# Attention over four batches at a time, one group of small products per chunk, ahead of two feed-forward layers on one Trainium2 core

## Chip, cores and metric

The kernel runs on one core of a Trainium2 chip. Its metric is the device time of one execution in microseconds (us). A run's figure is the median over repeated executions, and beside it stands one execution taken with the hardware profiler.

## What is computed

Linear attention with decay (batch B = 4, heads H = 8, sequence S = 768, head width D = 48) feeds two dense layers in fp32 accuracy; its rows become 3072 tokens of width 384.

```python
for t in range(S):
    cur = einsum('bhd,bhe->bhde', u * k[t], v[t])
    y[t] = einsum('bhd,bhde->bhe', r[t], state + cur)
    state = w * state + einsum('bhd,bhe->bhde', k[t], v[t])
x = y.transpose(0, 2, 1, 3).reshape(3072, 384)
h = x @ w_in            # 384 -> 2048
x = (h * cos(h)) @ w_out
g, val = x @ w_gate, x @ w_val   # 384 -> 1536
out = (g * sigmoid(g) * val) @ w_out2
```

The state of one batch and head is a 48 x 48 matrix, and batches do not depend on one another.

## The kernel before, in words

**Attention in chunks.** 128 tokens of one batch make a chunk `c`; there are 24, numbered batch by batch, so chunks 0 to 5 are batch 0. `attn_load` (L226) brings two transfers per chunk: `ch` (r and k by channel, 448 KB) and `tk` (r, k and v by token, 608 KB). Heads go in four pairs `q` of two halves `g`; half 0 lies on partitions 0 to 47 and half 1 on 64 to 111. VectorE scales `ch` with the decay tables (`attn_scale`, L243) and makes the diagonal term (`attn_diag`, L248 to L251). ScalarE writes that diagonal into two `am` tiles (L274, eight instructions). TensorE makes, per chunk, four sorts of small fp32 products; each fp32 product stands in the trace as two records, so 16 records a sort:

- scores (L281): 48 rows of either half against 128 columns, half 0 into PSUM bank `a` and half 1 into bank `b`; VectorE then lays them over `am` above the diagonal (L284, twice).
- growth of the state (L292), into bank `a`; not for the last chunk of a batch.
- old state times r (L298), into bank `x`, with a block-diagonal state of 112 rows; not for the first chunk of a batch.
- output (L314): v times `am`, into bank `x` behind the former.

The state is scaled on ScalarE (L306, four instructions) and added to on VectorE (L310, twice). The result `xo` is copied to `st` (L318 for block 0; L320 and L321 as a high and a low part for later blocks), and SyncE's queue moves it into the block's `x` tile by six transfers for a part (L327 to L332).

**Token blocks.** Four chunks in sequence make a block of 512 tokens (`TB`), six blocks in all. Block 0 is multiplied in plain fp32 with `wf`; later blocks use three reduced-precision products with high and low parts (`mm3`, L170 to L174). The steps of the first layer are pairs (block j, f), f = 0 to 15: `f1_up` (L406) makes 128 features into bank `h` (two banks in turn), a chain of six elementwise instructions turns them into `gh` and `gl` (L420 to L426, L177, L180; in block 0 the last two are left out), and `f1_down` (L435), two steps later, adds them into the three banks `y`.

**Order.** `attn_block` is a generator with four stretches per chunk; `schedule` (L497) takes one stretch after each `f1_up`, so block j+1 is made during the 16 steps of block j, its last output in step 15. Block 0 is made ahead of all steps. `prefix` (L74) comes first: small tables, chunk 0, the raw weights of f = 0 and 1, and a flag on the decays, on which all engines branch. In block 0's steps `conv1` (L133) turns 64-bit weights into fp32 from two raw buffers of 768 KB, and in block 1's steps `split1` splits them into `wt` tiles. The tile framework sorts instructions of a stretch by their readiness at build time, so an engine's order is not quite the program's; each engine then runs its queue in order. The second layer (`f2_up`, `f2_down`) follows from about 545 us on.

Of the kernel before, what the change touches and what calls it, by code (L numbers as in the profile page):

```python
# [18 lines left out]
C = 128  # L19
# [5 lines left out]
G = 256  # L25
# [7 lines left out]
TOKW = 2 * DM + NP * VW  # L33
CHW = 2 * NP * C
# [8 lines left out]
NSLOT = 34  # L43


class Kernel:
# [27 lines left out]
    def prefix(self):  # L74
# [6 lines left out]
        r1 = r0 + CHW + TOKW  # L81
# [18 lines left out]
        w = self.rawbuf[0][0:1, 0:DM]  # L100
# [15 lines left out]
        nc.scalar.activation(out=w, in_=w, func=ACTF.Abs, bias=self.center[:, 0:1])  # L116
        nc.vector.tensor_reduce(out=mx, in_=w, axis=AX.X, op=ALU.max)
        nc.vector.tensor_scalar(out=self.flag, in0=mx, scalar1=0.5 * (self.w_max - self.w_min), scalar2=None,
                                op0=ALU.is_le)
        self.attn_tables(wch)  # L120
        self.attn_scale(0)
        self.attn_ptok()
        self.attn_diag(0)
        self.raw1(0)
# [17 lines left out]
    def bank(self, tag, bufs=1):  # L142
        return self.ps.tile([128, 512], F32, tag=tag, bufs=bufs, name=tag)

# [41 lines left out]
    def attn_open(self):  # L186
        self.ap_guard = self.tc.tile_pool(name="attn", bufs=1)
        self.ap = self.ap_guard.__enter__()
        self.state = None
    def attn_tables(self, wch):  # L190
        nc = self.nc
        pr, pk = self.pr, self.pk
# [6 lines left out]
        while n <= hc:  # L199
            sq = up[:, :, n // 2:n // 2 + 1]  # L200
            nc.vector.tensor_tensor(out=up[:, :, n:n + 1], in0=sq, in1=sq, op=ALU.mult)
            if n < hc:
                nc.vector.tensor_tensor(out=up[:, :, n + 1:2 * n], in0=up[:, :, 1:n],
                                        in1=up[:, :, n:n + 1].to_broadcast([ROWS, NP, n - 1]), op=ALU.mult)
            n *= 2
        nc.vector.reciprocal(out=pk[:, :, hc:C], in_=up[:, :, 1:hc + 1])
        nc.scalar.activation(out=pr[:, :, hc:C], in_=up[:, :, 0:hc], func=ACTF.Copy)
        nc.vector.tensor_copy(out=pk[:, :, 0:hc], in_=up[:, :, hc - 1::-1])
# [17 lines left out]
    def attn_load(self, c, at=None):  # L226
        if c >= NCH or c in self.chunks:
            return
        nc = self.nc
        if at is None:  # L230
            ch = self.ap.tile([ROWS, 2, NP, C], F32, tag="ch", bufs=2, name="ch")
            tk = self.ap.tile([128, TOKW], F32, tag="tk", bufs=2, name="tk")
        else:
            ch = at[0:ROWS, 0:CHW].rearrange("p (a n t) -> p a n t", a=2, n=NP)
            tk = at[:, CHW:CHW + TOKW]
# [3 lines left out]
                          tk[:, 2 * DM:].rearrange("p (n w) -> p n w", n=NP))  # L239

# [13 lines left out]
    def attn_chunk(self, c, x, exact):  # L254
        nc, ap = self.nc, self.ap
        mm = nc.tensor.matmul
        first = c % NC_B == 0
        last = c % NC_B == NC_B - 1
        off = (c % CPB) * C
        ch, rt, kt, v = self.chunks[c]  # L260
        rm, km = ch[:, 0], ch[:, 1]
        if c:
            self.attn_scale(c)
            self.attn_diag(c)
        at = self.at.pop(c)
        if not last:
            nc.vector.tensor_tensor(out=kt, in0=kt, in1=self.ptok, op=ALU.mult)
        self.attn_load(c + 1)
        am = []
        for g in range(2):  # L270
            t = ap.tile([128, NP, C], F32, tag="am", bufs=2, name="am")
            for q in range(NP):
                h = 2 * q + g
                nc.scalar.activation(out=t[:, q], in_=self.ident, func=ACTF.Copy, scale=at[:, h:h + 1])  # L274
            am.append(t)
        yield
        sc = [self.bank(b).rearrange("p (n t) -> p n t", n=NP) for b in "ab"]
        for q in range(NP):
            for g in range(2):
                rows = slice(g * 64, g * 64 + D)  # L280
                mm(sc[g][:, q], lhsT=km[rows, q], rhs=rm[rows, q], start=True, stop=True)  # L281
        mask = self.upper.rearrange("p (o t) -> p o t", o=1).to_broadcast([128, NP, C])
        for g in range(2):
            nc.vector.copy_predicated(am[g], mask, sc[g])  # L284
        yield
        xo = self.bank("x").rearrange("p (n t) -> p n t", n=NP)
        wide = (slice(0, 64), slice(64, VW))
        if not last:
            po = self.bank("a")[:, 0:NP * D].rearrange("p (n d) -> p n d", n=NP)
            for q in range(NP):  # L290
                for g in range(2):
                    mm(po[g * 64:g * 64 + D, q], lhsT=kt[:, (2 * q + g) * D:(2 * q + g + 1) * D],  # L292
                       rhs=v[:, q, g * 64:g * 64 + D], start=True, stop=True)
        old = self.state
        if not first:
            for q in range(NP):
                for g in range(2):
                    mm(xo[wide[g], q], lhsT=old[:, q, wide[g]], rhs=rm[:, q],  # L298
                       start=(q == 0), stop=False)
        if not last:  # L300
            self.state = ap.tile([ROWS, NP, VW], F32, tag="state", bufs=2, name="state")
            if first:
                nc.gpsimd.memset(self.state, 0.0)
            else:
                for q in range(NP):
                    nc.scalar.activation(out=self.state[:, q], in_=old[:, q], func=ACTF.Copy,  # L306
                                         scale=self.w128[:, q:q + 1])
            for g in range(2):
                sv = self.state[g * 64:g * 64 + D, :, g * 64:g * 64 + D]
                nc.vector.tensor_tensor(out=sv, in0=sv, in1=po[g * 64:g * 64 + D], op=ALU.add)  # L310
        yield
        for q in range(NP):
            for g in range(2):
                mm(xo[wide[g], q], lhsT=v[:, q, wide[g]], rhs=am[g][:, q],  # L314
                   start=(first and q == 0), stop=(q == NP - 1))
        st = ap.tile([ROWS, 2, NP, C], F32, tag="st", bufs=1, name="st")
        if exact:
            nc.scalar.activation(out=st[:, 0], in_=xo[0:ROWS], func=ACTF.Copy)  # L318
        else:
            nc.scalar.activation(out=st[:, 0].bitcast(F32R), in_=xo[0:ROWS], func=ACTF.Copy)  # L320
            nc.vector.tensor_tensor(out=st[:, 1].bitcast(F32R), in0=xo[0:ROWS], in1=st[:, 0], op=ALU.subtract)  # L321
        for i in range(1 if exact else 2):
            dst = x if exact else x[:, i].bitcast(F32)
            src = st[:, i]
            put = nc.sync.dma_start
            o = slice(off, off + C)
            put(out=dst[0:D, :, o], in_=src[0:D, 0:KT])  # L327
            put(out=dst[D:2 * D, :, o], in_=src[64:64 + D, 0:KT])
            put(out=dst[96:128, 0, o], in_=src[0:32, KT])
            put(out=dst[96:112, 1, o], in_=src[32:48, KT])  # L330
            put(out=dst[112:128, 1, o], in_=src[64:80, KT])
            put(out=dst[96:128, 2, o], in_=src[80:112, KT])  # L332
        yield

    def attn_block(self, j):
        x = self.xblk[j] = self.xf if j == 0 else self.x_tile()
        for i in range(CPB):
            yield from self.attn_chunk(j * CPB + i, x, j == 0)
# [48 lines left out]
    def general_block(self, j):  # L387
        nc = self.nc
        x = self.xblk[j] = self.xf if j == 0 else self.x_tile()
# [239 lines left out]
```

## Time and profile before

| | |
|---|---|
| median of 3 runs | 993.65 us (993.15 to 995.31) |
| profiled execution | 994.0 us |
| its span, first to last instruction | 992.2 us |
| mean granted TensorE clock | 0.990 of full speed |
| busy: TensorE, VectorE, ScalarE | 959.6, 577.6, 466.8 us |

Busy time of TensorE is a union of intervals whose ends are modelled, since its products overlap. Its rate is better read from start to start of records that follow each other. The stages are the stretch ahead of the first up product (to 46.7 us), block 0 (to about 152 us), blocks 1 to 5 (to about 547 us) and the second layer.

### The profile page before, as it was taken

What the parts mean: (1) busy time and instruction counts of PE and PEld (TensorE: products, weight loads), DVE (VectorE), ACT (ScalarE), POOL (GpSimd) and SP (SyncE); (2) the same over time, 40 slices, a digit from 0 to 9 for tenths busy, and PEclk for the clock granted to TensorE, in tenths of its full rate; (3) what the DMA queues carried; (4) which work ended last, traced back from release to release, by engine and by line L of the source; (5) the groups of instructions that cost most, each with busy time, mean ns of one, the idle gap of its engine ahead of it and who ended that gap; (6) DMA issues with size and microseconds to landing.
All of it is one profiled execution on the core that took longest, in us unless ns stands there. A gap on an engine that the chain in (4) does not pass through costs nothing.

```text
span 992.2 us, 13079 instructions
## 1 busy us (share of the span) xinstructions
PE 959.6 (97%) x4988; PEld 745.1 (75%) x4988; DVE 577.6 (58%) x932; ACT 466.8 (47%) x905; POOL 2.1 (0%) x8
## 2 busy tenths in 40 slices
PE   3899999999999999999899999999999999999997
PEld 2644447777777877877787888888888888888886
DVE  7878897666766667765699873333333333333332
ACT  5676866556555565655699762211211222212111
POOL 0000000000000000000000000000000000000000
PEclk9799999999999999999999999999999999999999
DMA  6675524225224132321763601101001001000001
GB/s 216 193 246 172 170 65 151 64 76 161 63 62 149 54 94 68 124 60 31 257 191 118 232 1 46 51 1 63 34 1 64 32 1 64 32 1 9 25 0 36
DMA packets 50393, 86.21 MB, mean 87 GB/s; under 512 B 7057, under 2 KB 24338, under 8 KB 50322
## 3 DMA queue, kind: packets, MB, share of 16 engines
q1 hardware_dynamic: 50322, 85.29, 27.0%
q8 instruction: 41, 0.67, 0.3%
q14 instruction: 30, 0.25, 0.1%
HBM read 62.46 MB, written 14.16 MB: 77 GB/s over the span
## 4 chain that ended last, share of the span: by engine, by line
PE 80%; DVE 7%; DMA 6%; SPq 2%; ACT 2%; issue 1%; ACTq 0%; DVEq 0%
PE y L172 10%; PE h L172 10%; PE h L173 10%; PE h L174 10%; PE y L173 10%; PE y L174 10%; DMA region<-in_w 2%; PE b L174 2%; PE a L174 2%; PE a L172 2%; PE b L172 2%; PE b L173 2%; PE a L173 2%; PE x L314 2%; DVE wt L180 2%
## 5 line engine op out<-in xcount | busy, mean ns | idle before, releaser
L172 PE MATMUL h<-x,wt 128*128 128x512 f32 x456 | 177.7, 392 | 4.0 <-DVE q L426 2.2
L173 PE MATMUL h<-x,wt 128*128 128x512 f32 x456 | 178.4, 391 | 1.1 <-DMA x<-st 1.1
L174 PE MATMUL h<-x,wt 128*128 128x512 f32 x456 | 177.5, 389 | 0.0
L472 DVE SCALAR_TENSOR_TENSOR t<-t,h 128x512 f32<-128x512 f32 x72 | 49.5, 688 | 163.3 <-ACT t L471 163.3
L471 ACT ACTIVATE t<-h 128x512 f32<-128x512 f32 x72 | 42.9, 596 | 164.3 <-PE h L174 164.3
L177 ACT ACTIVATE ah<-a 128x512 fp32r<-128x512 f32 x72 | 45.4, 631 | 133.7 <-DVE a L473 133.7
L172 PEld LDWEIGHTS h<-x,wt 128*128 128x128 f32 x456 | 85.2, 188 | 23.4 <-DVE q L426 3.3
L173 PEld LDWEIGHTS h<-x,wt 128*128 128x128 f32 x456 | 85.6, 188 | 20.1 <-issue 2.5
L174 PEld LDWEIGHTS h<-x,wt 128*128 128x128 f32 x456 | 85.6, 188 | 17.7 <-issue 0.2
L172 PE MATMUL y<-gh,wt 128*128 128x512 f32 x240 | 97.9, 409 | 0.0
L420 ACT ACTIVATE k<-h,quarter 128x512 int32<-128x512 f32 x96 | 65.5, 682 | 63.4 <-PE h L174 56.9
L173 PE MATMUL y<-gl,wt 128*128 128x512 f32 x240 | 94.0, 392 | 0.7 <-DVE gl L180 0.7
L174 PE MATMUL y<-gh,wt 128*128 128x512 f32 x240 | 93.6, 390 | 0.0
L422 ACT ACTIVATE k<-q,half_pi 128x512 f32<-128x512 f32 x96 | 69.1, 720 | 45.8 <-DVE q L421 45.6
L173 PE MATMUL y<-al,wt 128*128 128x512 f32 x216 | 84.1, 390 | 0.0
L172 PE MATMUL y<-ah,wt 128*128 128x512 f32 x216 | 84.0, 389 | 0.0
L174 PE MATMUL y<-ah,wt 128*128 128x512 f32 x216 | 84.0, 389 | 0.0
L421 DVE SCALAR_TENSOR_TENSOR q<-h,k 128x512 f32<-128x512 f32 x96 | 65.9, 686 | 27.1 <-ACT k L420 26.5
L180 DVE TENSOR_TENSOR gl<-q,gh 128x512 fp32r<-128x512 f32 x80 | 55.1, 690 | 37.6 <-ACT gh L177 37.1
L180 DVE TENSOR_TENSOR al<-a,ah 128x512 fp32r<-128x512 f32 x72 | 49.8, 692 | 46.2 <-ACT ah L177 46.1
L426 DVE TENSOR_TENSOR q<-h,k 128x512 f32<-128x512 f32 x80 | 55.1, 689 | 16.5 <-ACT k L422 15.0
L274 ACT ACTIVATE am<-region,at 128x128 f32<-128x128 f32 x192 | 62.0, 391 | 5.3 <-PE x L314 4.0
(106 smaller groups left out, 1543.9 us busy)
## 6 DMA issues: line engine op xcount, KB each, us to landing
tk<-in_rkv_tok SPq DMA_DIRECT2D x23, 608.0 KB, 4.4
raw<-in_w SPq DMA_DIRECT2D x36, 384.0 KB, 4.3
region<-in_w SPq DMA_DIRECT2D x16, 768.0 KB, 5.4
ch<-in_rk_ch SPq DMA_DIRECT2D x23, 448.0 KB, 3.8
y_scratch<-region SPq DMA_DIRECT2D x36, 256.0 KB, 3.3
x<-y_scratch SPq DMA_DIRECT2D x12, 768.0 KB, 5.7
x<-st SPq DMA_DIRECT2D x80, 72.0 KB, 2.9
out<-region SPq DMA_DIRECT2D x18, 256.0 KB, 2.1
```

Source lines behind the costliest of these rows:

```text
L172: mm(out, lhsT=lh, rhs=rh, start=start, stop=False)
L173: mm(out, lhsT=lh, rhs=rl, start=False, stop=False)
L174: mm(out, lhsT=ll, rhs=rh, start=False, stop=stop)
L177: self.nc.scalar.activation(out=hi, in_=src, func=ACTF.Copy)
L180: self.nc.vector.tensor_tensor(out=lo, in0=src, in1=hi.bitcast(F32), op=ALU.subtract)
L274: nc.scalar.activation(out=t[:, q], in_=self.ident, func=ACTF.Copy, scale=at[:, h:h + 1])
L420: nc.scalar.activation(out=ki, in_=h, func=ACTF.Identity, scale=INV2PI, bias=self.quarter[:, 0:1])
L421: nc.vector.scalar_tensor_tensor(out=q, in0=h, scalar=INV2PI, in1=ki, op0=ALU.mult, op1=ALU.subtract)
L422: nc.scalar.activation(out=k, in_=q, func=ACTF.Sin, scale=TWOPI, bias=self.half_pi[:, 0:1])
L426: nc.vector.tensor_tensor(out=q, in0=h, in1=k, op=ALU.mult)
L471: nc.scalar.activation(out=t, in_=gate, func=ACTF.Tanh, scale=0.5)
L472: nc.vector.scalar_tensor_tensor(out=t, in0=t, scalar=1.0, in1=gate, op0=ALU.add, op1=ALU.mult)
```

## The change

**Chunks by time.** `layouts` orders chunks by time block first: chunk c is batch c mod 4 and time block c // 4. A block of 512 tokens is now the same 128 tokens of all four batches, so its four chunks are independent of one another, and each needs the state of its batch four chunks back. Chunks 0 to 3 have no old state and chunks 20 to 23 no growth. The host turns the result back.

**One group per chunk.** The generator is replaced by a table of steps. In one step, behind its `f1_up`: output of chunk n, old state, growth and the state's update, then the scores of chunk n+1; scaling, diagonal and mask lie one or two steps before or after. Groups are three steps apart; the block's last output is in step 14 of block 0 and in step 13 of each later block.

**State.** It holds 48 columns, four tiles for the four batches, and old-state products take 48 rows by 48 columns of each half, both halves into bank `x`. Growth goes into the bank that the next `f1_up` will use. The update is two VectorE instructions over 112 partitions.

**Block 0.** Chunks 1 to 4 are all loaded at once (1 and 2 into the buffers of `x`), two sets of score and output banks alternate, and no state is needed; growth of chunks 0 to 3 follows the first `f1_up`.

**x in place.** ScalarE and VectorE write three head pairs straight into `x`; the fourth goes through `st` and six transfers per chunk for both parts together. `NSLOT` falls from 34 to 33.

```diff
-NSLOT = 34
+NSLOT = 33
...
-        self.attn_load(0, first)
+        self.attn_load(0, first[0:ROWS, 0:CHW], first[:, CHW + FIRST:])
+        nc.sync.dma_start(out=self.u_tok, in_=a["u_tok"])
         nc.sync.dma_start(out=self.ident, in_=a["ident"])
-        nc.sync.dma_start(out=self.u_tok, in_=a["u_tok"])
         nc.sync.dma_start(out=self.upper, in_=a["upper"])
-        for f in range(1, NRAW):
-            self.raw1(f)
+        self.raw1(0)
...
+    def attn_out(self, c, bank="x"):
...
+        for q in range(NP):
+            for g in range(2):
+                mm(xo[wide[g], q], lhsT=v[:, q, wide[g]], rhs=am[g][:, q],
+                   start=(q == 0), stop=(first and q == NP - 1))
+        if first:
+            return
+        st = self.state[c % CPB]
+        for q in range(NP):
+            for g in range(2):
+                rows = slice(g * 64, g * 64 + D)
+                mm(xo[rows, q], lhsT=st[rows, q], rhs=ch[rows, 0, q], start=False, stop=(q == NP - 1))
...
+    def attn_state(self, c):
+        tt = self.nc.vector.tensor_tensor
+        st, po = self.state[c % CPB], self.po.pop(c)[0:ROWS]
+        if c < CPB:
+            self.nc.vector.tensor_copy(st, po)
+            return
...
+        tt(out=st, in0=st, in1=w128, op=ALU.mult)
+        tt(out=st, in0=st, in1=po, op=ALU.add)
+
+    def attn_store(self, c):
...
+        if c < CPB:
+            nc.scalar.activation(out=x[0:ROWS, :, o], in_=xo[:, 0:KT], func=ACTF.Copy)
+            nc.scalar.activation(out=st[:, 0], in_=xo[:, KT], func=ACTF.Copy)
...
+        for kt in range(KT):
+            for g in range(2):
+                rows = slice(g * 64 + D, g * 64 + 64)
+                src = slice(g * 64 + 16 * kt, g * 64 + 16 * kt + 16)
+                if c < CPB:
+                    nc.sync.dma_start(out=x[rows, kt, o], in_=st[src, 0])
+                else:
+                    nc.sync.dma_start(out=x[rows, :, kt, o].bitcast(F32), in_=st[src])
+
+    def attn_first(self):
+        self.xblk[0] = self.xf
+        for c in (1, 2):
+            self.attn_load_early(c)
+        self.raw1(1)
+        self.attn_load(3)
+        self.attn_load(4)
+        scores, out = ("ab", ("y0", "y1")), ("x", "y2")
+        for c in range(CPB):
...
+            self.attn_scores(c, scores[c % 2])
+            if c:
+                self.attn_mask(c - 1)
+                self.attn_out(c - 1, out[(c - 1) % 2])
+                self.attn_store(c - 1)
+            if c < 2:
+                self.conv1(c)
...
+    def attn_begin(self):
...
+                self.attn_ptoks(c)
+                self.attn_grow(c, bank[:, i * 256:i * 256 + NP * D])
+        for c in range(CPB):
+            self.attn_state(c)
+        self.attn_load(5)
...
+        def group(c, n):
+            if n >= 0:
+                self.attn_out(n)
+                if n < NCH - CPB:
+                    self.attn_grow(n, self.next_h()[:, 0:NP * D])
+                    self.attn_state(n)
+            if c is not None:
+                self.attn_scores(c)
+            if n >= 0:
+                self.attn_load(n + 2)
+                if n % CPB == 0:
+                    self.xblk[n // CPB] = self.x_tile()
+                self.attn_store(n)
+        at(0, self.attn_begin)
+        for j in range(1, NB):
+            t0 = (j - 1) * NF1 + (2 if j == 1 else 1)
+            for i in range(CPB):
+                c, t = j * CPB + i, t0 + 3 * i
...
+                at(t, group, c, c - 1 if i else -1)
+                at(t + 1, self.attn_mask, c)
+            at(t0 + 3 * CPB, group, None, c)
...
             self.f1_up(j, f)
-            next(attn, None)
+            for fn in plan.get(i, ()):
+                fn[0](*fn[1:])
```

## Rows read from the trace of the kernel before

**Rows 1.** The profile's page: TensorE's busy line and the chain that ended last.
```profile
PE 959.6 (97%) x4988; PEld 745.1 (75%) x4988; DVE 577.6 (58%) x932; ACT 466.8 (47%) x905; POOL 2.1 (0%) x8
...
PE 80%; DVE 7%; DMA 6%; SPq 2%; ACT 2%; issue 1%; ACTq 0%; DVEq 0%
```

**Rows 2.** Busy time by stretch: length, engines, granted clock, DMA share, GB/s.
```profile
120.00:140.00 20.00, 20.00 (x102) 9.76 (x102) 19.88 (x39) 17.14 (x41) 0.00 (x0) 1.00 0.20 59
...
540.00:560.00 20.00, 19.30 (x85) 15.26 (x84) 17.02 (x32) 16.20 (x31) 0.00 (x0) 1.00 0.96 348
```

**Rows 3.** Timeline of TensorE, first stage: start us, us, what, count, idle before.
```profile
17.13 1.93 PE L314 MATMUL x<-am,region 128*64 128x128 f32 x16
...
46.67 5.42 PE L414 MATMUL h<-region,wf 128*128 128x512 f32 x12
52.02 0.64 PE L314 MATMUL x<-am,tk 128*48 128x128 f32 x6
52.59 0.37 PE L281 MATMUL a<-ch 48*128 48x128 f32 x1
...
52.80 0.27 PE L281 MATMUL a<-ch 48*128 48x128 f32 x1
...
54.66 2.84 PE L414 MATMUL h<-region,wf 128*128 128x512 f32 x6 [1.14 <-DVE gf L426]
```

**Rows 4.** Timelines of VectorE, ScalarE and SyncE, and landings, first stage.
```profile
14.55 1.23 DVE L243 TENSOR_TENSOR ch<-ch,region 112x1024 f32<-112x1024 f32 x1 [3.29 <-DMA ch<-in_rk_ch]
...
10.59 2.44 ACT L274 ACTIVATE am<-region,at 128x128 f32<-128x128 f32 x8
...
42.91 0.65 SPq L327 DMA_DIRECT2D region<-st  x1
...
x<-st SPq DMA_DIRECT2D x80, 16.0 KB, 1.8
```

**Rows 5.** Groups by form: busy us, mean ns of one, idle before.
```profile
L249 DVE TENSOR_TENSOR tk<-tk 128x384 f32<-128x384 f32 x23 | 12.8, 556 | 0.6
...
L284 DVE COPY_PREDICATED am<-region,a 128x512 f32<-128x512 uint32 x24 | 17.5, 729 | 1.8 <-PE b L281 1.8
...
L310 DVE TENSOR_TENSOR state<-state,a 48x192 f32<-48x192 f32 x40 | 14.0, 351 | 12.6 <-PE a L292 12.0
...
L422 ACT ACTIVATE k<-q,half_pi 128x512 f32<-128x512 f32 x96 | 69.1, 720 | 45.8 <-DVE q L421 45.6
...
L177 ACT ACTIVATE gh<-q 128x512 fp32r<-128x512 f32 x80 | 49.9, 625 | 29.4 <-DVE q L426 29.3
```

**Rows 6.** Timeline of TensorE in block 1, scores between large products.
```profile
169.16 0.39 PE L174 MATMUL h<-x,wt 128*128 128x512 f32 x1
169.47 0.37 PE L281 MATMUL a<-ch 48*128 48x128 f32 x1
...
169.69 0.27 PE L281 MATMUL a<-ch 48*128 48x128 f32 x1
...
170.36 0.27 PE L281 MATMUL b<-ch 48*128 48x128 f32 x1
170.57 0.50 PE L172 MATMUL y<-gh,wt 128*128 128x512 f32 x1
170.90 0.39 PE L173 MATMUL y<-gl,wt 128*128 128x512 f32 x1
```

**Rows 7.** The same timeline: growth and old state, then the large products.
```profile
174.87 0.56 PE L292 MATMUL a<-tk 128*48 128x48 f32 x16
175.27 1.05 PE L298 MATMUL x<-ch,state 112*64 112x128 f32 x16
176.25 0.50 PE L172 MATMUL y<-gh,wt 128*128 128x512 f32 x1
```

**Rows 8.** Waits of TensorE from 468 to 487 us: total, times, longest.
```profile
PE h L172 <- DVE q L426: 1.7, 1, 1.7
PE h L173 <- DMA x<-st: 0.8, 1, 0.8
```

More of the change, by code (lines that the diff above doesn't have):

```diff
@@ L33 @@
 TOKW = 2 * DM + NP * VW
+FIRST = 128
 CHW = 2 * NP * C
@@ L252, in attn_diag, with attn_am, attn_ptoks, attn_scores @@
         self.at[c] = at
[L254 to L264, printed above, removed]
+    def attn_am(self, c):
         at = self.at.pop(c)
[L266 to L269, printed above, removed]
+        self.am[c] = []
         for g in range(2):
-            t = ap.tile([128, NP, C], F32, tag="am", bufs=2, name="am")
+            t = self.ap.tile([128, NP, C], F32, tag="am", bufs=4, name="am")
             for q in range(NP):
                 h = 2 * q + g
[L274 to L277, printed above, removed]
+                self.nc.scalar.activation(out=t[:, q], in_=self.ident, func=ACTF.Copy, scale=at[:, h:h + 1])
+            self.am[c].append(t)
+    def attn_ptoks(self, c):
+        kt = self.chunks[c][2]
+        self.nc.vector.tensor_tensor(out=kt, in0=kt, in1=self.ptok, op=ALU.mult)
+    def attn_scores(self, c, banks="ab"):
+        ch = self.chunks[c][0]
+        sc = self.sc[c] = [self.bank(b).rearrange("p (n t) -> p n t", n=NP) for b in banks]
         for q in range(NP):
@@ L280, in attn_chunk, with attn_mask @@
                 rows = slice(g * 64, g * 64 + D)
-                mm(sc[g][:, q], lhsT=km[rows, q], rhs=rm[rows, q], start=True, stop=True)
+                self.nc.tensor.matmul(sc[g][:, q], lhsT=ch[rows, 1, q], rhs=ch[rows, 0, q], start=True, stop=True)
+    def attn_mask(self, c):
         mask = self.upper.rearrange("p (o t) -> p o t", o=1).to_broadcast([128, NP, C])
[L283 to L286, printed above, removed]
-        wide = (slice(0, 64), slice(64, VW))
[L288 to L311, printed above, removed]
+        for am, sc in zip(self.am[c], self.sc.pop(c)):
+            self.nc.vector.copy_predicated(am, mask, sc)
+    def attn_out(self, c, bank="x"):
+        mm = self.nc.tensor.matmul
+        ch, v = self.chunks[c][0], self.chunks[c][3]
+        am = self.am.pop(c)
+        first = c < CPB
+        wide = (slice(0, 64), slice(64, VW))
+        xo = self.xo[c] = self.bank(bank).rearrange("p (n t) -> p n t", n=NP)
         for q in range(NP):
@@ L322, in attn_chunk @@
[L322 to L332, printed above, removed]
@@ new lines, in general_first, with general_plan @@
+    def general_first(self):
+        self.xblk[0] = self.xf
+        for kt in range(KT):
+            self.general_part(0, kt)
+        self.raw1(1)
+        for f in range(2):
+            self.conv1(f)
+    def general_plan(self):
+        plan = {}
+        for j in range(1, NB):
+            for kt in range(KT):
+                plan[(j - 1) * NF1 + 2 + kt] = [(self.general_part, j, kt)]
+            plan[(j - 1) * NF1 + 2].insert(0, (lambda i: self.xblk.update({i: self.x_tile()}), j))
+        return plan
@@ L409, in f1_up @@
         w = self.w1[f][0]
-        h = self.bank("h", 2)
+        h = self.next_h()
+        self.nh += 1
         for kt in range(KT):
@@ L502, in schedule @@
         a = self.a
+        self.nh = 0
         if fast:
             self.attn_open()
-        block = self.attn_block if fast else self.general_block
-        for _ in block(0):
-            pass
-        nconv = nsplit = 0
+            self.attn_first()
+            plan = self.attn_plan()
+        else:
+            self.general_first()
+            plan = self.general_plan()
+        nconv, nsplit = 2, 0
         steps = [(j, f) for j in range(NB) for f in range(NF1)]
@@ L511, in schedule @@
             if f == 0:
-                attn = block(j + 1) if j + 1 < NB else iter(())
                 if j == NB - 1:
```

145 lines of the change are left out of this document (91 added, 54 removed).

## The prediction

> **What bounds the kernel now.** I read the page first, then busy time by stretch, then TensorE's timeline from start to start of its records. The page says TensorE: 97% busy and 80% of the chain that ended last [rows 1]. So a gain must come from three places: time before TensorE is gapless, time it spends on small products and on changing over to them, and gaps in its stream. The timeline of the first stage shows where gaplessness begins: the first up product of block 0 starts at 46.67, the last break ends at 54.66, and by then two features' up products, all of chunk 4 (its last output records stand at 52.02) and the scores of chunk 5 (52.59) are done [rows 3]. In block 0 TensorE is full, and VectorE nearly so (19.88 of 20 us from 120 to 140) [rows 2]. The page's sums say nothing of the first stage or of changes between sorts of products; the timelines do.
>
> **Prices on TensorE.** In block 1, scores stand between large products [rows 6]. From 170.90 to the next small product at 174.87 [rows 7] lie 17 large ones, so one takes 0.23 us. A pair of score records takes 0.11 (169.69 to 170.36 is six pairs), so the 16 records of a sort own 0.88. From 169.16 to 170.90 pass 1.74: two large products (0.46), the scores' 0.88, and 0.40 that belongs to the two changes, 0.20 each. Growth followed by old state takes 0.40 and 0.98 with no change visible between them [rows 7]; less half a change at either end, growth owns 0.30 and old state 0.88, and I give output the 0.88 of the same count and columns. A full chunk before is three groups: 3 x 0.88 + 0.30 + 6 x 0.20 = 4.14 us.
>
> **Part 1, the first stage.** What the old kernel has done at 54.66 costs 5.35 (two up products, 46.67 to 52.02 [rows 3]) + 4.14 + 1.1 (scores and one change) = 10.6. The new one, which does none of it earlier, is level if its up products start at 54.66 - 10.6 = 44.1. Growth of chunks 0 to 3, 4 x 0.30 and two changes, 1.6, moves behind the first up product; scheduled into the gap before it, it would be free, and I charge half, 0.8. When do the up products start? The last chunk needs its `tk`. Before, chunk 1's `ch` was there at 14.5 [rows 4], when 3360 KB had been asked for since 1.6: 260 KB/us. Up to chunk 3's `tk` the new order asks for 6080 KB (four chunks of 1056, two raw weights of 768, tables of 320): 23.4 us, so 25.0. At the best stretch's rate, 348 GB/s [rows 2], it is 17.9, so 19.5. The queue is now filled without breaks but in the same stage; I take 23.5. Behind it, one after the other: diagonal 3 x 0.56 [rows 5], `am` 2.44 [rows 4], two masks 1.46 [rows 5], output 1.93, which is what it took in the first stage at the low one of TensorE's two clock levels (1.2 of 2.4 GHz) [rows 3], two copies of together 512 columns about 0.9 (one of 512 takes 0.63 [rows 5]), and two transfers, 0.65 each to issue and 1.8 to land [rows 4]: 11.5, so 35.0. VectorE has for three chunks 3 x (1.23 + 1.7 + 1.46) = 13.2 us and two weight conversions in that time; I add 2 for its queue and 1 for up products that start at the low clock: 38. Gain: 44.1 - 38 - 0.8 = **5.3 us**. Bounds: 19.5 and no queue give 32 and a gain of 11; 25.0 and a queue of 5 give 43 and none.
>
> **Part 2, one group per chunk.** For chunks 4 to 23 the old kernel pays 20 x 4.14, less three old-state sorts (chunks 6, 12 and 18 begin a batch) and four growths (5, 11, 17, 23): 82.8 - 2.6 - 1.2 = 79.0. The new one pays 20 x 2.64 + 16 x 0.30 = 57.6 for the products, since in chunks 4 to 23 every one has an old state now and chunks 20 to 23 lack growth. Changes: old-state products become 48 x 48 in either half, growth and output stay 128 rows high, scores are 48 rows by 128. So out to state, state to growth, growth to scores each change the shape; no row shows these three. The nearest rows bound one from 0 (growth to old state, same shape [rows 7]) to 0.20. Output to scores at 52.02 changes the shape within attention, and its first pairs stand 0.21 apart against 0.11 [rows 3], as at an entry; so I take 0.20. A block has groups with 2, 3 x 5 and 4 changes, the last block 2, 3 x 4 and 3: 4 x 21 + 17 = 101, 20.2 us. Sum 77.8, **gain 1.2 us**; with inner changes free, 25 groups x 2 x 0.20 = 10, sum 67.6 and a gain of 11.4. The Trainium skill (TensorEngine Tiling (Array Packing), Tiling Modes, Key Properties) says that changing the tiling mode, not the tile alone, drains TensorE: by that the inner changes cost and the gain is 1.2, though no run here shows those three.
>
> **Part 3, gaps at block ends.** Into block 5 TensorE waited 1.7 for a late elementwise chain and 0.8 for the last transfers of `x` [rows 8]. The last output now comes two steps earlier; a step of 18 products took 4.30 with one change (170.57 to 174.87 [rows 6, 7]), so 8 us, more than six transfers and a landing (6 x 0.65 + 1.8 = 5.7 [rows 4]). **Gain 2.5 us.** I give nothing for the gap into block 1: VectorE is full there [rows 2], from weight splits as much as from attention. Bounds: 0 to 7.
>
> **Part 4, a new wait.** Growth now sits in the bank of the next up product. That product waits until VectorE has added it to the state, and VectorE's queue holds the current up product's chain ahead of that: six instructions of 0.63 to 0.72 [rows 5], 4.1, plus two state instructions near 0.35 [rows 5], 4.8 in all. TensorE meanwhile runs the group (2.94 + 5 x 0.20 = 3.9) and one down product of nine (2.1): 6.0. So 1.2 us of cover is left; one mask or scaling in between eats it. I charge **2 us** for 16 groups; ends 0 and 16 (one more VectorE instruction than the cover holds, 1 us each). Queued behind that wait on TensorE is everything else.
>
> **Edits at nothing.** ScalarE loses four state scalings per chunk and gains one short copy; VectorE's update stays two instructions; SyncE's queue issues six transfers per chunk in place of twelve. None ends the chain in gapless stretches, and TensorE covers them; without that cover each costs under 1 us a chunk. One slot less leaves 33 of 33 tiles in block 1's splits: a raw weight may load later, with half the kernel to spare.
>
> **Sum.** 5.3 + 1.2 + 2.5 - 2 = 7.0. The profiled execution took 994.0 around a span of 992.2; so 987.0, and 0.35 less for the median of 993.65: **986.5 us**, with 978 to 993 of its own from the bounds of parts 1 and 3.
>
> **Rivals.**
> - *Slower: the halves of the old state run one after the other.* Now both row halves write one bank; before, the only products from two row halves, the scores, went into two banks, and pairs at 0.11 [rows 6] show only that case. If such a pair does not overlap, each of 20 chunks pays 0.88 more: 17.6, so 1004. It decides from 0.35 a chunk on (7.0 over 20). For: the bank pair of the scores. Against: the output partitions are apart too, as in L298. The Trainium skill (TensorEngine Tiling (Array Packing), Restrictions and Gotchas, Gotcha 1) says that different row tiles cannot access one PSUM bank at once; read as a serial order, that is this rival, and no run here shows it.
> - *Slower too: the bank wait costs 1 us each*, 16 in place of 2: 1001. VectorE's load speaks for it; 1.2 us of cover against.
> - *The first stage is no shorter*: transfers and VectorE's queue hold up products to 43, the gain of 5.3 is gone: 992.
> - *Inner changes are free*, as between growth and old state [rows 7]: 10.2 more, so 977; with an early start, 971.
>
> **Chances.** Forecast 0.52, free changes 0.20, first stage no shorter 0.12, serial halves 0.10, bank wait 0.06. About 0.2% (2 us) is what a measurement can tell from no change. Faster by more: 0.50 of the forecast, 0.20, and 0.05 of the third, 0.75; within it: 0.02 and 0.07, 0.09; slower: 0.10 and 0.06, 0.16. The range 971 to 999 leaves out serial halves, part of the bank waits and the tail of the early ones, under 0.2.
>
> **What would show it.** Right: up products start at 36 to 40 us and run without breaks; old-state records pair at 0.11; the group takes 3.9 with first pairs at 0.2 after each change; no wait into block 5. Wrong: a start past 43; old-state records 0.11 apart singly, 1.8 a sort; TensorE waiting for VectorE's state add ahead of L414 or L172 in `h`; or a group near 3.1.

## The result, and the profile after

| | before | after |
|---|---|---|
| median of the runs beside each other | 993.68 us (993.15 to 995.31, 4 runs) | 984.84 us (983.06 to 986.74, 4 runs) |
| ratio, 95% interval | | 0.9909 (0.9881 to 0.9936) |
| profiled execution, its span | 994.0, 992.2 | 986.74, 984.9 |

The forecast was 986.5 and faster. The time came out 1.7 us from it, but not by its terms. The page of after, against [rows 1] (the last line is an issue: kernel side, count, size, median us to landing):

```profile
PE 954.8 (97%) x4988; PEld 750.3 (76%) x4988; DVE 574.3 (58%) x947; ACT 449.1 (46%) x866; POOL 0.2 (0%) x4
...
PE 88%; DVE 4%; DMA 3%; ACT 2%; issue 1%; SPq 1%; ACTq 0%; DVEq 0%
...
x<-st SPq DMA_DIRECT2D x120, 16.0 KB, 1.8
```

The page puts TensorE at the same 97% with the same 4988 records, as before. To see where 7.3 us of the profiled execution went, take the same marks on TensorE's timeline in both: the third feature's up product of block 0, the first down product of each later block, the second layer's first product into bank `a`, and the last product. At the first mark both have done the scores and outputs of chunks 0 to 4 and the scores of chunk 5; chunk 4's growth, 0.6 us with its change (priced below), stands ahead of that mark before and behind it after.

| mark, us | before | after | stretch that ends there, after minus before |
|---|---|---|---|
| third up product of block 0 | 54.66 | 56.36 | +1.7 |
| first down product of block 1 | 155.73 | 155.11 | -2.3 |
| first down product of block 2 | 239.88 | 236.40 | -2.9 |
| of block 3 | 322.48 | 317.69 | -1.3 |
| of block 4 | 404.34 | 398.98 | -0.6 |
| of block 5 | 485.29 | 478.38 | -1.5 |
| second layer | 547.75 | 540.44 | -0.4 |
| last product | 986.39 | 979.08 | 0.0 |

So the first stage got longer, by 1.7 us and with chunk 4's growth by some 2.3, not 5.3 us shorter; the blocks gave everything, 6.7 us of it in blocks 1 to 5.

**The first stage.** TensorE's timeline of after (start us, us, what, count, idle before and its releaser), against [rows 3]:

```profile
30.04 1.94 PE L300 MATMUL y<-am,tk 128*48 128x128 f32 x14 [0.39 <-DVE am L289]
...
43.28 1.94 PE L300 MATMUL x<-am,tk 128*48 128x128 f32 x14 [1.02 <-DVE am L289]
45.15 0.66 PE L308 MATMUL x<-ch,state 48*48 48x128 f32 x2
45.74 7.08 PE L514 MATMUL h<-region,wf 128*128 128x512 f32 x12
52.76 1.07 PE L308 MATMUL x<-ch,state 48*48 48x128 f32 x14
...
56.36 2.84 PE L514 MATMUL h<-region,wf 128*128 128x512 f32 x6 [1.45 <-DVE gf L526]
```

Chunk 3's output is done at 32.0, where the forecast has it at 33 (35.0 less 4.0 for copies and transfers, plus 2 for VectorE's queue). The first up product still starts at 45.74. ScalarE's and SyncE's queues show what came between:

```profile
32.99 0.27 ACT L338 ACTIVATE st<-x 112x128 f32<-112x128 f32 x1
33.15 0.98 ACT L271 ACTIVATE am<-region,at 128x128 f32<-128x128 f32 x3
...
36.47 1.00 ACT L157 ACTIVATE cvu<-region,low_bias 128x768 uint32<-128x768 uint32 x1
37.35 0.29 ACT L338 ACTIVATE st<-y 112x128 f32<-112x128 f32 x1
```

```profile
17.75 6.65 SPq L350 DMA_DIRECT2D region<-st  x6
...
27.49 13.84 SPq L350 DMA_DIRECT2D region<-st  x18
```

Chunk 3's copy to `st` could run from 32.3 on, when chunk 1's last transfer out of the same buffer had landed, and ran at 37.35: ScalarE's queue holds `am` of chunk 4 and a weight conversion ahead of it. Its six transfers were the last of the 18 to be issued, up to 41.33; the last issue began at 40.7 and took 1.8 to land. The first up record needs only the first two of the six, which fill its part of `x`: in five kernels below it starts 0.41 to 0.46 us after the second has landed. Here that one landed at 39.96, so the start would have been 40.4, 2.4 later than forecast. The other 5.3 us come from TensorE's own queue: chunk 4's output stood ahead of the up product and waited for its two masks, up to 43.23. The six of chunk 0, issued from 17.75 behind loads on SyncE's queue, took 8.4 us in the median to land; all 24 of this stage:

```profile
DMA to landing us min/median/max: 1.6/1.8/9.9
```

The windows of after (length; busy us of TensorE, its weight loads, VectorE, ScalarE, GpSimd; granted clock; DMA share; GB/s), against [rows 2], show a stage that is full of transfers and then empty:

```profile
10.00:30.00 20.00, 12.94 (x101) 9.98 (x98) 18.57 (x28) 14.92 (x42) 0.00 (x0) 0.97 0.99 325
30.00:40.00 10.00, 7.40 (x89) 6.43 (x89) 6.31 (x13) 6.51 (x17) 0.00 (x0) 0.56 0.05 10
...
45.00:50.00 5.00, 5.00 (x10) 2.12 (x9) 1.23 (x1) 0.00 (x0) 0.00 (x0) 0.59 1.01 390
```

From 30 to 40 the DMA engines move 10 GB/s and TensorE is not full; from 45 to 50 its granted clock is 0.59, mostly the 1.2 GHz level, after that broken stretch. So the first 12 up records took 7.02 from start to start (45.74 to 52.76), against 5.35 before.

**The groups.** TensorE's timeline in block 1 of after, against [rows 6, 7]:

```profile
163.37 1.09 PE L300 MATMUL x<-am,tk 128*64 128x128 f32 x16
164.39 1.08 PE L308 MATMUL x<-ch,state 48*48 48x128 f32 x16
165.39 0.67 PE L317 MATMUL h<-tk 128*64 128x48 f32 x16
165.99 0.37 PE L284 MATMUL a<-ch 48*128 48x128 f32 x1
...
167.08 0.50 PE L173 MATMUL y<-gh,wt 128*128 128x512 f32 x1
167.42 0.39 PE L174 MATMUL y<-gl,wt 128*128 128x512 f32 x1
```

The 16 old-state records take 1.00 (164.39 to 165.39), though both halves write one bank. From the first output record to the first large product pass 3.71. A large product takes 0.23, and two changes stretch the last one ahead and the first behind: 0.09 more from 163.05 to 163.37, 0.11 more from 167.08 to 167.42. That is 3.9 for a group. The longer waits of TensorE from 55 to 155 us (total, times, longest) are the charged one, for the state, and the break at 56.36:

```profile
PE h L514 <- DVE state L328: 1.6, 2, 0.8
PE h L514 <- DVE gf L526: 1.4, 1, 1.4
```

In blocks 1 to 5 there is no TensorE wait for the state. There is one other, ahead of block 5's first down product, which waits for its bank `y` to be read out; the forecast had no wait there:

```profile
PE y L173 <- DVE region L551: 1.7, 1, 1.7
```

**The block ends.** What the old kernel paid there shows between two blocks, in the rows without a wait. TensorE's timeline of before at the end of block 1's steps:

```profile
226.47 0.37 PE L281 MATMUL a<-ch 48*128 48x128 f32 x1
...
227.53 0.70 PE L172 MATMUL h<-x,wt 128*128 128x512 f32 x2
228.16 0.37 PE L281 MATMUL a<-ch 48*128 48x128 f32 x1
...
228.58 0.50 PE L172 MATMUL y<-gh,wt 128*128 128x512 f32 x1
...
230.85 0.47 PE L292 MATMUL a<-tk 128*48 128x48 f32 x10
231.25 0.50 PE L173 MATMUL h<-x,wt 128*128 128x512 f32 x1
...
235.11 0.33 PE L292 MATMUL a<-tk 128*48 128x48 f32 x5
```

The next block's `x` is not there, and the queue is built around that: scores split into 12 and 4 records, growth into 10, 5 and 1, and down products go ahead of up products. Each split is one more pair of changes. By count of the records, the stretches of blocks 1 to 4 have 34, 34, 32 and 20 changes before, and 21, 21, 21 and 15 after. Among growth, old state and output of the old kernel a change shows no price (0.40 and 0.98 in [rows 7]); without these, 29, 27, 27 and 18 are left.

### The profile page after: what moved, and what is told of

It reads as the page before. It is cut to its first block, busy times and chain, and to the rows that moved or that the text cites. A ratio compares the mean times of both kernels' runs of the same rounds, so it can differ in the third digit from the quotient of the medians.

```text
span 984.9 us, 12840 instructions
## 1 busy us (share of the span) xinstructions
PE 954.8 (97%) x4988; PEld 750.3 (76%) x4988; DVE 574.3 (58%) x947; ACT 449.1 (46%) x866; POOL 0.2 (0%) x4
## 4 chain that ended last, share of the span: by engine, by line
PE 88%; DVE 4%; DMA 3%; ACT 2%; issue 1%; SPq 1%; ACTq 0%; DVEq 0%
PE y L173 11%; PE y L174 10%; PE h L173 10%; PE h L175 10%; PE h L174 10%; PE y L175 10%; PE h L514 3%; PE b L174 2%; PE a L174 2%; PE b L175 2%; PE a L175 2%; PE a L173 2%; PE b L173 2%; PE y L543 2%; PE x L300 2%; PE x L308 2%
## 5 line engine op out<-in xcount | busy, mean ns | idle before, releaser
L173 PE MATMUL y<-gh,wt 128*128 128x512 f32 x240 | 95.6, 400 | 1.8 <-DVE region L551 1.7
L175 PE MATMUL y<-gh,wt 128*128 128x512 f32 x240 | 93.6, 390 | 0.0
```

What stands on the lines that cost most here:

```text
L173: mm(out, lhsT=lh, rhs=rh, start=start, stop=False)
L175: mm(out, lhsT=ll, rhs=rh, start=False, stop=stop)
```

## The experiments

Every kernel ran beside the kernel before on its chip, and ratios are to that. Block times are between the marks of the table above.

**Undo the new timing alone.** The groups stay, and the last output goes back to step 15.

```diff
-            t0 = (j - 1) * NF1 + (2 if j == 1 else 1)
+            t0 = (j - 1) * NF1 + 3
```

> The changed kernel with its groups one step (block 1) or two steps (blocks 2 to 5) later, so that each block's last output is made in step 15, as in the kernel before. The number of groups and of changes stays. Theory A (what blocks 1 to 5 gained is mostly that the next block's x is there in time, 1.5 to 2.5 us at each block end): 6 to 8 us slower than the changed kernel, 991 to 993, with TensorE waiting at the ends of blocks for x or for the elementwise chain. Rival (the gain is the smaller number of changes): no difference, 984.8, and blocks at 81.29 us.

Measured: 990.78 us, ratio 0.9963 (0.9949 to 0.9976). Blocks 1 to 5 take 390.58, 5.25 more than after's 385.33. Waits of TensorE from 155 to 487 us:

```profile
PE h L173 <- DVE q L526: 4.7, 4, 1.7
```

A wait for the elementwise chain, as in [rows 8], stands at four block ends. At the end of block 1 the last transfers of `x` are issued from 226.37, the next block's up product starts only at 230.50, behind a row of down products, and the third up product from there waits 1.08 for the chain (237.26), since hardly a down product is left to stand between them. So most of the gain of blocks 1 to 5 is the earlier last output.

**The timing alone, without the change.** Two stretches of attention more in the first two steps of each block, in the kernel before.

```diff
             self.f1_up(j, f)
             next(attn, None)
+            if f < 2:
+                next(attn, None)
```

> The kernel before with one edit: in the first two steps of a block two stretches of the attention are taken in place of one, so that the block's last output is made in step 13 in place of 15; groups and changes stay as they were. Theory A (late x at block ends costs the kernel before 1.5 to 2.5 us a block, 3 to 4 into blocks 1 and 5): 5 to 7 us faster than before, 987 to 989. Rival (the gain is the smaller number of changes): within 1 us of before, 993.7.

Measured: 985.98 us, ratio 0.9915 (0.9902 to 0.9928), the change's own within the intervals. Blocks 1 to 5 take 384.25 against 392.03 of before. In the stretch of block 2 (four outputs, old states and growths in both kernels) it takes 81.57, after 81.29. Its blocks 1 to 3 have 25, 27 and 25 changes in place of 34, 34 and 32 (22 each without those that show no price). Block 0 gains nothing by it, 101.33 against 101.07. From 155 to 487 us TensorE no longer waits for the chain or for `x`, only for the banks `y`:

```profile
PE y L172 <- DVE region L451: 3.5, 3, 2.8
```

So one edit without groups, order of chunks or `x` in place gives a gain as large as the whole change's; grouping is worth 0.28 us a block there.

**Order within a group.** Output, growth, old state: two products of like shape (128 rows high) stand side by side.

```diff
                 self.attn_out(n)
                 if n < NCH - CPB:
                     self.attn_grow(n, self.next_h()[:, 0:NP * D])
...
+                self.attn_old(n)
+                if n < NCH - CPB:
                     self.attn_state(n)
```

> The changed kernel with one edit: in a group the old-state products come behind growth, so output and growth, which have the same shape on TensorE, stand side by side, and a group has four changes of shape in place of five. Theory A (a change costs 0.2 us wherever it stands): the 16 groups with growth each lose one change, 3.2 us; a full block of the first layer takes 80.5 in place of 81.29, growth's 16 records shrink from 0.59 to about 0.4, and the time is 981.6. Rival (inner changes are free and the 0.2 belong to entering and leaving the group): nothing moves, 984.8.

TensorE's timeline, one group:

```profile
248.10 1.09 PE L300 MATMUL x<-am,tk 128*64 128x128 f32 x16
249.02 0.62 PE L318 MATMUL h<-tk 128*48 128x48 f32 x16
249.57 1.08 PE L309 MATMUL x<-ch,state 48*48 48x128 f32 x16
250.58 0.37 PE L284 MATMUL a<-ch 48*128 48x128 f32 x1
```

Output to scores takes 2.48, in after 2.62 (163.37 to 165.99): 0.14 less, not 0.20. The time did not follow: 986.21 us, ratio 0.9918 (0.9902 to 0.9933). Blocks 1 to 5 take 384.06, 1.3 less than after, but 1.1 of that is block 4, which in the change itself takes 79.40 in one profile and 78.60 in another; blocks 1 to 3 give only 0.2 where twelve groups at 0.14 would give 1.7. The first stage came out later (block 0's first down product at 62.41 instead of 59.04). In block 3, which takes 81.63 where after has 81.29, two of the up products behind a group start 0.15 after the state's addition and some 0.3 late (367.47 and 383.30), and one wait stands in the trace:

```profile
PE h L173 <- DVE state L329: 0.2, 1, 0.2
```

In blocks 1 to 3 the addition now ends 0.15 to 1.0 us ahead of the up product, in after 0.4 to 2.5. With it later, part of the saving goes back to the wait that the forecast had charged. Why the first stage came out later stays open.

**How much cover the bank wait has.** Six more copies of the state onto itself ahead of the update, on VectorE.

```diff
         tt = self.nc.vector.tensor_tensor
...
+        for _ in range(6):
+            self.nc.vector.tensor_copy(st, st)
         tt(out=st, in0=st, in1=w128, op=ALU.mult)
```

> The changed kernel with six extra copies of the state onto itself (112 x 192, about 0.35 us each, 2.1 us a chunk) ahead of each state update of chunks 4 to 19; the numbers computed stay the same. It doubles and more the time until the bank of the next up product is free. Theory A (the cover is the 1.2 us of the forecast): TensorE waits for the state's addition ahead of an up product in most of 16 groups, about 0.9 us each, and the kernel is 10 to 15 us slower. Rival (the build order puts the addition ahead of the current feature's last instructions, so the cover is larger): under 4 us slower, no wait of TensorE for the state in blocks 1 to 5.

Measured: 995.27 us, ratio 0.9997 (0.9978 to 1.0016), 0.0088 more than the change's ratio, 8.7 us of 994, between the two theories. Six copies of 0.25 and what the framework's order puts between them move the addition from 247.67 in after to 257.33 here, where the group itself starts 5.0 us later: 4.6 us within the group. VectorE and TensorE of after, then VectorE and TensorE of this kernel:

```profile
247.67 0.34 DVE L328 TENSOR_TENSOR state<-state,h 112x192 f32<-112x192 f32 x1
...
248.45 0.69 DVE L181 TENSOR_TENSOR gl<-q,gh 128x512 fp32r<-128x512 f32 x1
```

```profile
250.54 0.39 PE L173 MATMUL h<-x,wt 128*128 128x512 f32 x1
```

```profile
257.33 0.36 DVE L330 TENSOR_TENSOR state<-state,h 112x192 f32<-112x192 f32 x1
```

```profile
257.84 0.47 PE L173 MATMUL h<-x,wt 128*128 128x512 f32 x1
```

In after the addition ends at 248.01, 2.5 us ahead of the up product. Here the up product comes 0.15 behind the addition, with 18 down products between group and up product instead of 9; so it does in nine of the twelve groups of blocks 1 to 3. The list of waits has three of these, together 1.3 us:

```profile
PE h L173 <- DVE state L330: 1.3, 3, 0.6
```

So the wait is real and decides once its cover is gone. By the profiles blocks 1 to 3 take 6.7 us longer than in after; the nine late up products account for 3.1 of that, from start to start of records, two more changes a block (23 instead of 21) for 1.2, and the rest is not traced to a cause. Block 0 takes 3.8 longer, and block 4, which has no state to update, 1.9 less.

**Chunk 4's load late.** Chunk 4 is loaded behind the first stage's four chunks, so that its work no longer stands ahead of theirs.

```diff
         self.attn_load(3)
-        self.attn_load(4)
...
+        self.attn_load(4)
```

> The changed kernel with chunk 4's two loads (1056 KB) issued with chunk 5's, behind the first up product, in place of ahead of block 0. Theory A (the first stage was lengthened by loads that stand ahead of chunk 0's small transfers, which took 9.9 us to land, and by chunk 4's output, which stood ahead of the first up product and waited for its masks until 43.2): the first up product starts at 39 to 42 in place of 45.7, chunk 4's 4 us come later, and the time is 0 to 3 us faster. Rival (the start is set by SyncE's 24 transfers of 0.64 us and by the reuse of st alone): the start moves by less than 2 us and the kernel is 2 to 4 us slower, 987 to 989.

TensorE's timeline:

```profile
38.05 5.75 PE L514 MATMUL h<-region,wf 128*128 128x512 f32 x12 [1.58 <-DMA region<-st]
44.88 0.34 PE L284 MATMUL a<-ch 48*128 48x128 f32 x1 [1.08 <-DVE ch L253]
...
48.63 5.08 PE L514 MATMUL h<-region,wf 128*128 128x512 f32 x6 [2.82 <-DVE gf L526]
```

Measured: 983.72 us, ratio 0.9886 (0.9871 to 0.9902). The up product starts at 38.05, as forecast for the change itself; chunk 3's second transfer landed at 37.59. Of these 7.7 us block 1's first down product keeps 1.9 (153.20): VectorE's queue has chunk 4's scaling ahead of the current up product's chain and waits for its load, TensorE waits 2.82 for `gf`, and the granted clock falls to 0.64 from 45 to 50.

**Chunk 4's load in the middle**, in the third chunk's turn, behind the second chunk's small transfers.

```diff
-        self.attn_load(4)
...
+            if c == 2:
+                self.attn_load(4)
```

> The changed kernel with chunk 4's two loads behind the second chunk's small transfers on the queue, between the order of the changed kernel (ahead of all) and that of the run with chunk 4 loaded late. Theory A (ahead of all they delay the transfers; loaded late they leave VectorE waiting 4.5 us for chunk 4 in front of the first feature's elementwise chain): the first up product at 38 to 41, chunk 4's products done early as well, and 982 to 983. Rival (chunk 4's output in front of the first up product is what holds it): start near 45, 984 to 986.

TensorE's timeline:

```profile
39.09 0.34 PE L284 MATMUL a<-ch 48*128 48x128 f32 x1 [3.81 <-DVE ch L253]
...
40.18 7.11 PE L515 MATMUL h<-region,wf 128*128 128x512 f32 x12
47.23 1.09 PE L300 MATMUL x<-am,tk 128*64 128x128 f32 x16
```

Measured: 982.32 us, ratio 0.9861 (0.9839 to 0.9883); up product at 40.18, chunk 4's output behind it at 47.23, block 1's first down product at 150.44, 4.7 earlier than after. What holds the start here is chunk 4's scores, which wait for its scaling; chunk 3's second transfer had landed at 37.54. So chunk 4's work ahead of the up product held the start in after, and when that work comes decides how much of the early start is kept.

**Block 0's small transfers on GpSimd's queue.**

```diff
-                    nc.sync.dma_start(out=x[rows, kt, o], in_=st[src, 0])
+                    nc.gpsimd.dma_start(out=x[rows, kt, o], in_=st[src, 0])
```

> The changed kernel with block 0's 24 small transfers of the fourth head pair issued on GpSimd's queue in place of SyncE's, where they stood among the loads. Theory A (the fourth pair's path, that is issue at 0.64 us each, waiting behind loads of the same queue, and through the reuse of the two st buffers the copies on ScalarE, holds x of block 0 until 42.5 us): x is complete 3 to 5 us earlier; since chunk 4's output still stands ahead of the first up product on TensorE until its masks at 43.2, the start moves by 0 to 2 us and the time by as much. Rival (the queue does not matter, the transfers themselves are slow while loads run): chunk 0's transfers still take near 10 us to land and the start stays at 45.7.

TensorE's timeline, and the landings of the 24 transfers:

```profile
39.13 8.11 PE L514 MATMUL h<-region,wf 128*128 128x512 f32 x12 [2.76 <-ACT cvu L157]
47.17 1.09 PE L300 MATMUL x<-am,tk 128*64 128x128 f32 x16
```

```profile
DMA to landing us min/median/max: 1.5/5.3/6.7
```

Measured: 982.32 us, ratio 0.9856 (0.9835 to 0.9877); block 1's first down product at 149.96, 5.2 earlier than after. More than was expected: not because each transfer lands sooner (the median rose from 1.8 to 5.3, the longest fell from 9.9 to 6.7). Two other things changed with the queue: chunk 3's copy to `st` runs at 34.42, not 37.35, and its second transfer lands at 38.72, 1.2 earlier than in after; and the build put chunk 4's output behind the first up product (47.17), which takes out the 5.3 us that it held in after. So an early start does not need chunk 4's load to be late. No run had the one without the other.

**Load in the middle and GpSimd's queue together, and with the order of the group on top.** The edits are those shown above; the change as it is ran beside them.

> The changed kernel as it is, beside the next two. Both theories: 983 to 987 on the chip of before's 994, the first up product at 45 to 46, first down product of block 1 near 155.1, blocks 1 to 3 at 81.3 each. A start several us off these would say that the first stage varies by itself, and then the gains of the kernels with an edited first stage are to be doubted.

> Both edits of the first stage that each brought the first down product of block 1 to 150.4 and 150.0: chunk 4's load between the second and third chunk's work, and block 0's 24 small transfers on GpSimd's queue. Theory A (two causes of the late start, loads ahead of the transfers and chunk 4's scaling ahead of the last copies, that add): first up product at 36 to 38, first down product of block 1 near 147, 978 to 980. Rival B (each edit takes out the same hold, and behind it stands a next one, VectorE's queue or the masks): first up product at 39 to 40, 149.5 to 150.5, 981 to 983.

> As the run before, and in each group output, growth, then old state, so that the two shapes alike stand side by side. Theory A: the group is 0.14 shorter, 16 times, 2 us less than the run before, the other stages equal. Rival B: as when the order was changed alone, the build order of the first stage shifts and takes it back: within 1 us of the run before or slower.

Measured: the change 985.59 us, ratio 0.991 (0.9888 to 0.9933), block 1's first down product at 153.71 (155.11 in the first profile), blocks 1 to 3 again 81.29 each. So the time up to block 1 varies by over a microsecond by itself (0.7 each in the first stage and in block 0), and the late load's 1.9 is not far above that; the 4.7 and 5.2 of the other two are. Both edits 982.94, ratio 0.9877 (0.9851 to 0.9903), block 1's first down product at 152.51, later than with either edit alone: they do not add. Nor was chunk 4's load in the middle in this kernel: with the small transfers off SyncE's queue the build issued it at 15.34 and 23.95, where the run with the load in the middle has 29.55 and 30.18. The up product starts at 39.73, and what it waits for is still a transfer of `st`; its first 12 records then take 8.1, at the low clock from 40 to 45. TensorE's timeline and that window:

```profile
39.73 8.17 PE L515 MATMUL h<-region,wf 128*128 128x512 f32 x12 [2.23 <-DMA region<-st]
```

```profile
40.00:45.00 5.00, 5.00 (x7) 1.91 (x7) 2.47 (x3) 1.39 (x5) 0.00 (x0) 0.50 0.66 227
```

With the order of the group on top, 979.12 us, ratio 0.9838 (0.9815 to 0.9862): the fastest median measured, 6.5 us under the change on the same chip. The expected 2 us on top came out as 3.8, but not where they were expected: blocks 1 to 3 take 243.76 instead of 243.86, and block 1's first down product comes at 148.46 instead of 152.51. Of these 4.05 us the start of the up product gives 1.0 (38.72), its first 12 records 1.1 (7.02 instead of 8.10, at a granted clock of 0.67 instead of 0.50 from 40 to 45), and block 0 2.0 (99.16 instead of 101.11). Which of that is due to the edit and which to the run isn't settled.

**Late load, GpSimd's queue and order of the group**, three of the edits above at once.

> The changed kernel with three edits at once: output, growth, old state in that order within a group; chunk 4's loads issued with chunk 5's; block 0's small transfers on GpSimd's queue. Theory A: each keeps its own effect, about 1.3 us in blocks 1 to 5 from the order, 2 us or more from the first stage: 979 to 982, faster than every kernel so far. Rival (the build order of the first stage shifts with each edit and gives back what the edits bring): 983 to 986.

Measured: 981.17 us, ratio 0.9841 (0.9818 to 0.9864), up product at 40.30, block 1's first down product at 151.24. No better than the one before it, and like it below the change with its whole interval, as no other run of an edited first stage but that with GpSimd's queue alone is. In this kernel too chunk 4's loads were issued at 15.63 and 24.24, not late.

## Why the prediction was right in its sum and wrong in its terms

**Part 1, +5.3 forecast, -1.7 measured.** The step that failed is "behind it, one after the other": two copies, two transfers, 11.5 us, plus 2 for VectorE's queue. The chunk's own work came as costed (`tk` there at 22.5, output done at 32.0). But the step assumed that the fourth chunk's tail runs as soon as its inputs are there, and that the up product follows at once. The `st` copy stood 5 us behind `am` of chunk 4 and a conversion on ScalarE, which cost 2.4 of the start; chunk 4's output stood ahead of the up product on TensorE, which cost 5.3. Chunk 4, loaded "all at once" with the others, had no place in the sum. The late load shows it: with chunk 4 gone the up product starts at 38.05, the forecast's 38. The 1 us for "up products that start at the low clock" was too little as well: the first 12 records took 7.02 in place of 5.35 in after, and up to 8.10 with an early start. In the run with the late load 1.9 us were left of 7.7, as chunk 4's work and the low clock followed. The growth that was charged with 0.8 did fit into the gap (35.55 to 39.1). The rival of a first stage no shorter was right in that, and wrong in its time, 992, since it kept the other terms.

**Part 2, 1.2 forecast, about 1 measured.** A group takes 3.9 as forecast. Inner changes cost 0.20: a block's 81.29 less 288 large products at 0.2267 and four groups of products at the forecast's 2.94 leaves 4.2 us for 21 changes. So the rival of free changes is out. Growth, priced at 0.30, takes 0.60 with its change (165.39 to 165.99), so 0.40 by itself, 0.1 too little in each of 16 groups; output and old state, 1.02 and 1.00 with a change where 1.08 was taken, make up for it. The block 2 stretch without groups against with them (81.57 and 81.29) puts grouping at 0.28 a block, 1.1 in four blocks. The Trainium skill (TensorEngine Tiling (Array Packing), Tiling Modes, Key Properties) has a drain on a change of the mode, and none on a change of tile within it: the run with output and growth side by side saves 0.14 of 0.20, which agrees with the direction and leaves 0.06 that it does not explain.

**Part 3, 2.5 forecast, the largest gain by measurement.** "I give nothing for the gap into block 1" and nothing for those into blocks 2 to 4 is the step that failed. The view that was read, waits of TensorE, holds 2.5 into block 5 and only 0.8 more from 155 us on; at the other block ends the loss stands in the timeline as split groups, down products ahead of up products, and changes (29 with a price in block 1 against 21). Late outputs alone cost 5.25 us in the blocks of the new kernel, and early ones alone win 7.8 in those of the old. The step's own size, six transfers and a landing inside two steps, was right: no TensorE wait for `x<-st` is left.

Into block 1 the old kernel's one long wait was for weights, and its granted clock was 0.79 and 0.87 from 140 to 150 behind it:

```profile
PE h L172 <- ACT wt L177: 1.6, 1, 1.6
```

After has no such wait, and a clock of 1.00. The early output alone did not bring that (block 0 took 101.33); which part of the change did stays open.

**Part 4, -2 forecast, -1.6 measured, all of it in block 0.** There the addition ends 0.05 us ahead of the up product in two of four groups. In the twelve groups of blocks 1 to 3 the cover is 0.4 to 2.5 us, 2.35 in the median, where the forecast had 1.2: in the group shown the build put the state's addition ahead of the current chain's last instruction, not behind the whole chain. The mechanism is right, as the six copies show.

**Rivals.** Old-state halves overlap in one bank: 16 records in 1.00, so 0.10 a pair once a change of 0.20 is off. The Trainium skill (TensorEngine Tiling (Array Packing), Restrictions and Gotchas, Gotcha 1) rules out that row tiles access one bank at once; read as a serial order it is not what this trace shows, where the two halves write different partitions of the bank.

So 5.3 that did not come and 1.7 that were lost were made up in the blocks. These gave 9.0. Of the 6.7 in blocks 1 to 5 the late output alone takes back 5.25, and grouping is about 1.1; the 2.3 in block 0 came although 1.6 was paid there for the state. That the terms add up to within 1.7 us of the measured time is luck: the largest was off by 7.0 one way, and what the block ends gave above their 2.5, with block 0, made that good. Of the forecast's own signs of being wrong two came true, a start past 43 and a wait for the state's addition. Its bounds are loosely added: parts 1 and 3 together allow 976 to 994, not 978 to 993; both hold the measured time.

## What to carry to other kernels

When one stage feeds the next through transfers, look at the boundaries in the timeline, not only at the waits: a scheduler that sees a late input hides the wait by reordering, and the loss shows as split groups and changes of shape. Costing a critical tail by its own durations gives the earliest end only; whatever the same engines have queued for later work belongs in the sum. And measure the cheapest part alone: here a two-line edit of the old kernel gave as much as the whole rewrite.

## What the runs showed of the hardware

- A transfer of 8 KB issued behind loads of 400 to 768 KB took up to 9.9 us to land, and 1.8 otherwise; on GpSimd's queue at most 6.7. The Trainium skill (DMA: Bandwidth & Descriptors, Queues, rings and completion order) says that each DMA engine consumes one queue's descriptors in order and takes turns between queues, which agrees with the longest landing, and does not give the median, which rose to 5.3.
- One change of shape on TensorE takes 0.20, of which 0.09 lies ahead of the new shape's first record and 0.11 behind it; between output and growth, both 128 rows high, some 0.06 is left of it.
- An early start does not bring full speed: in all six kernels whose up products started at 38 to 40.3 the stretch from 40 to 50 held five microseconds at a granted clock of 0.50 to 0.67. An fp32 record of 512 columns then takes 0.85 us from start to start, 0.43 at the full clock.
